# A transformer block's backward pass on one core: sixteen row gathers issued from SyncE's queue, with the order and the homes of buffers searched again

## The chip, the cores and the metric

The kernel runs on one core of a Trainium2 chip. The metric is device time of one execution in microseconds, lower is better. The profile speaks of five engines: PE (TensorE, the matrix multiplier; PEld is its weight load, which overlaps it), DVE (VectorE), ACT (ScalarE), POOL (GpSimd) and SP (SyncE, which computes nothing and only issues transfers). Transfers run on 16 DMA engines that all queues share; "DMA share" is their mean busy time in units of one full set, and can read a little above 1.

## The reference

One block over 2048 rows of 512 numbers in bfloat16, forward and backward: layer norm, attention in which each row looks at 8 rows before it at a distance of 2 (32 heads of 16), a residual, layer norm, a feed-forward net 512 to 1792 to 512 with gelu, a residual. The outputs are the block's result and the gradients of x, wqkv, wo, w1, b1, w2 and b2.

```python
def _A_ref(x, wqkv, wo):
    H = 32; Dh = D // H
    W, dil = 8, 2
    qkv = (x @ wqkv).reshape(B, S, 3, H, Dh).transpose(2, 0, 3, 1, 4)
    q, k, v = qkv[0], qkv[1], qkv[2]
    idx = arange(S)[:, None] - (arange(W) * dil)[None, :]
    mask = idx >= 0
    kg, vg = k[:, :, idx_c], v[:, :, idx_c]
    logits = einsum("bhsd,bhswd->bhsw", q, kg) * Dh ** -0.5
    attn = softmax(where(mask, logits, -1e9))
    o = einsum("bhsw,bhswd->bhsd", attn, vg)
    return o.transpose(0, 2, 1, 3).reshape(B, S, D) @ wo
h = x + _A_ref(layernorm(x), wqkv, wo)
h2 = h + gelu(layernorm(h) @ w1 + b1) @ w2 + b2
# the kernel gives h2 and, for a given grad_out, the gradients of
# x, wqkv, wo, w1, b1, w2, b2
```

## The kernel before

The 2048 rows are cut into four chunks of 512. For each chunk the forward pass makes layer norm, q, k and v, the attention's weights, its output `o`, and the feed-forward net; then come the backward parts of the net, of the attention and of layer norm; products for the weight gradients (`wg_group`) are spread between them and give PE work while others wait.

Nothing in the kernel sets its order by the place in the code. A `Plan` (L62) records 1948 operations, each with an engine, the buffers it reads and writes, and so its predecessors. `emit` (L118) then writes them out in the order of a table, `ORDER`, and lays each buffer at the address that a second table, `HOMES`, gives it. Memory is used many times over: an operation that writes a buffer waits for all that used the same addresses before. Each engine, and SP's and POOL's sequencers among them, runs its own operations strictly in that order. 276 operations are SP's and 33 POOL's.

Attention over 8 rows at distance 2 is done by a *gather* (L456): one transfer that gives each of 128 partitions 18 neighbouring rows of 512 numbers from a tensor in DRAM, 2304 KB in all, as one long piece of 18432 bytes per partition (L460). There are 16: rows of v for the forward output (`Ro`, from `p1_o`, L705, one for each chunk) and, in `p3_bands` (L925), rows of k, go and q for the gradients of q, v and k (`Rq`, `Rv`, `Rk`, one each for each chunk). A gather can leave when its rows stand in DRAM and the memory of its buffer is free. What then uses it is `band` (L501), four times for each gather: DVE multiplies the rows by coefficients (`prbo`, `prbq`, `prbv`, `prbk`, L507), PE sums the products into PSUM (the band sum, L516, eight matmuls with `S4`), ACT writes them out (L521), and `turn` (L525, PE at L532) transposes two of them.

Other names: loads are issued at L282, stores at L287, transposing loads at L291, stores of transposed blocks at L445, all from SP unless they say otherwise. POOL issues, besides the gathers, four stores of `ost` to `o_d` and three stores of `gqs`, `gvs` and `gks` (L287). L297 is ACT's eviction of PSUM. `mmul` is a matmul, as one piece (L270) or as four of 32 columns (L268). `wg_group` (L977) evicts two blocks of a weight gradient into one buffer `wgs` and stores it in 256 KB (`out_dram<-wgs`). `ln1b` (L953) are the rows of layer norm that the last backward part reads, loaded in four pieces per chunk. `ln1T`, `ln2T` and `qt` are transposed rows that feed the matmuls of the first 130 us.

Of the kernel before, what the change touches and what calls it, by code (L numbers as in the profile page):

```python
# [10 lines left out]
P = 128  # L11
# [21 lines left out]
def _ap(apobj, dims, off=0):  # L33
    return bass.AP(tensor=apobj.tensor, offset=apobj.offset + off, ap=[list(d) for d in dims])
# [125 lines left out]
def kernel(  # L160
# [21 lines left out]
    V, A, T, G, SY = nc.vector, nc.scalar, nc.tensor, nc.gpsimd, nc.sync  # L182
# [4 lines left out]
    S, D = xf.shape  # L187
# [11 lines left out]
    RW = 18  # L199
# [44 lines left out]
    sb, ps_, op, fx = pl.sb, pl.ps, pl.op, pl.fixed  # L244
# [211 lines left out]
    def gather(d_b, c, back, tag, soft=()):  # L456
        R = sb("R" + tag, [P, RW, 512])
        r0 = c * CH + (RPAD - 14 if back else 0)
        n = ((c - 1, 1) if c else "b") if back else ((c + 1, 0) if c + 1 < NC else "b")
        op("POOL", 0.58, lambda: G.dma_start(out=R().rearrange("p a d -> p (a d)"), in_=_ap(d_b()[r0:r0 + 1, :], [[4 * D, P], [1, RW * D]])),  # L460
           r=[(d_b, (c, 0)), (d_b, (c, 1)), (d_b, n)] + ([(d_b, (c - 1, 0))] if back and c else []), w=[R], dma=GATHER, tag="gather" + tag, soft=soft, piece=0.8, mode=4)
        return R
# [858 lines left out]
```

## Time and profile before

| | us |
|---|---|
| median of 3 runs | 568.17 (566.8 to 573.35) |
| profiled execution, its own time | 562.53 |
| its span | 560.8 |
| mean granted clock of TensorE | 0.983 |

The profiled execution is one more run; its time is a little below the three others. The span lies 1.7 us inside the time. Of the span, the first 126 us hold the forward pass up to the feed-forward net, then its forward and backward parts follow to about 308 us, then weight gradients of the net with the attention's backward part between them, and from 546 us on the last stores. The transfers by line, with KB and the median from issue to landing:

```profile
Ro<-v_d POOLq DMA_DIRECT2D x4, 2304.0 KB, 11.3
Rq<-k_d POOLq DMA_DIRECT2D x4, 2304.0 KB, 10.9
Rv<-go_d POOLq DMA_DIRECT2D x4, 2304.0 KB, 13.2
```

### The profile page before, as it was taken

To read this page: it belongs to the slowest core of one execution; us is meant where nothing else is said; L and a number is where in the kernel's file an instruction comes from. 1 tells how busy PE (TensorE), PEld (TensorE's weight loads), DVE (VectorE), ACT (ScalarE), POOL (GpSimd) and SP (SyncE) were. 2 spreads that over 40 slices of the span, in tenths; PEclk is the share of its full clock that TensorE was granted. 3 is DMA by queue.
4 is the path that set the end of the run, shared out by engine and by line. 5 is a ranking of instruction groups with operands and counts; after the bars stand their busy time and mean duration, and the time that the engine had idled before them with its cause. 6 is when DMAs were issued, how large, how long until landed. Compare 5 with 4: busy or idle time off the path is not lost. (4 is left out here: it accounts for less than half of the span.)

```text
span 560.8 us, 12918 instructions
## 1 busy us (share of the span) xinstructions
PE 535.7 (96%) x5479; PEld 270.5 (48%) x5512; DVE 494.5 (88%) x649; ACT 306.0 (55%) x480; POOL 24.7 (4%) x38
## 2 busy tenths in 40 slices
PE   8999879999999999999999999999986999999996
PEld 4966434444544444444444444465443554555542
DVE  7999999999999998899895096999984999999984
ACT  3975358988999848892441314213112475554332
POOL 1300100020001000000000000000010001000000
PEclk9999979999999999999999999999997999999999
DMA  8999999998998695669999999999995999659456
GB/s 267 241 318 274 333 280 377 201 285 219 278 221 224 190 238 152 166 150 197 261 187 199 229 202 217 293 200 310 220 399 238 315 315 314 290 197 229 105 145 174
DMA packets 218122, 135.32 MB, mean 241 GB/s; under 512 B 168464, under 2 KB 213712, under 8 KB 216016
## 3 DMA queue, kind: packets, MB, share of 16 engines
q1 hardware_dynamic: 214752, 93.07, 73.0%
q0 software_dynamic: 3312, 41.42, 19.1%
q8 instruction: 43, 0.70, 0.5%
q14 instruction: 15, 0.12, 0.1%
HBM read 55.74 MB, written 39.40 MB: 170 GB/s over the span
## 5 line engine op out<-in xcount | busy, mean ns | idle before, releaser
L270 PE MATMUL ps<-goT,w2T 128*128 128x512 bf16 x220 | 53.5, 379 | 0.5 <-DVE r L699 0.4
L297 ACT CAST wgs<-ps 128x512 bf16<-128x512 f32 (+1 forms) x30 | 16.3, 560 | 66.8 <-PE ps L268 29.0
L270 PE MATMUL ps<-w,gl 128*128 128x512 bf16 x215 | 52.1, 379 | 0.5
L270 PE MATMUL ps<-w1T,xb 128*128 128x512 bf16 x219 | 51.7, 379 | 0.3
L468 DVE TENSOR_TENSOR prb<-got,vw 128x4096 bf16<-128x4096 bf16 x16 | 36.0, 2285 | 16.7 <-ACT got L297 16.4
L270 PE MATMUL ps<-ln2T,w 128*128 128x512 bf16 x192 | 46.8, 390 | 0.3 <-DVE xb L848 0.3
L507 DVE TENSOR_TENSOR prbq<-Rq,cfq 128x4096 bf16<-128x4096 bf16 x16 | 36.1, 2278 | 9.0 <-PE ps L516 7.3
L766 ACT ACTIVATE xb<-ps,b1c 128x512 bf16<-128x512 f32 x56 | 35.4, 693 | 12.5 <-DMA g_d<-gl 9.0
L848 DVE SCALAR_TENSOR_TENSOR xb<-xb,ps 128x512 bf16<-128x512 bf16 x56 | 37.2, 681 | 5.5 <-PE ps L270 4.6
L507 DVE TENSOR_TENSOR prbv<-Rv,cfv 128x4096 bf16<-128x4096 bf16 x16 | 36.0, 2284 | 1.6 <-DMA Rv<-go_d 1.5
L507 DVE TENSOR_TENSOR prbk<-Rk,cfk 128x4096 bf16<-128x4096 bf16 x16 | 35.9, 2286 | 1.5 <-PE ps L516 1.2
L507 DVE TENSOR_TENSOR prbo<-Ro,cfo 128x4096 bf16<-128x4096 bf16 x16 | 36.0, 2285 | 1.2 <-PE ps L476 1.1
L468 DVE TENSOR_TENSOR prf<-qt,kt 128x4096 bf16<-128x4096 bf16 x16 | 35.6, 2282 | 0.0
L270 PEld LDWEIGHTS <-xb 128*128 128x128 bf16 x224 | 21.9, 98 | 26.4
L270 PEld LDWEIGHTS <-gl 128*128 128x128 bf16 x224 | 21.5, 98 | 26.9 <-ACT gl L769 1.0
L270 PEld LDWEIGHTS <-w2T 128*128 128x128 bf16 x220 | 21.4, 98 | 26.8 <-issue 1.5
L616 PE MATMUL ps<-ln1T,wqk 128*32 128x512 bf16 x512 | 31.1, 382 | 1.3 <-DVE ln1T L301 1.0
L270 PE MATMUL ps<-gor,gw2in 128*128 128x512 bf16 x129 | 30.6, 379 | 0.3 <-issue 0.2
L270 PEld LDWEIGHTS <-w 128*128 128x128 bf16 x192 | 19.0, 100 | 24.5 <-issue 3.7
L550 ACT ACTIVATE gyr<-ps,rstd 128x512 bf16<-128x512 f32 x16 | 10.9, 682 | 34.2 <-PE ps L270 34.2
L268 PE MATMUL ps<-gw1in,ln 128*32 128x512 bf16 x464 | 28.8, 396 | 0.0
L788 ACT ACTIVATE xb<-xb 128x2048 bf16<-128x2048 bf16 (+1 forms) x16 | 26.9, 1692 | 2.4 <-DVE xb L787 2.4
(194 smaller groups left out, 1028.4 us busy)
## 6 DMA issues: line engine op xcount, KB each, us to landing
Ro<-v_d POOLq DMA_DIRECT2D x4, 2304.0 KB, 11.3
Rq<-k_d POOLq DMA_DIRECT2D x4, 2304.0 KB, 10.9
Rv<-go_d POOLq DMA_DIRECT2D x4, 2304.0 KB, 13.2
Rk<-q_d POOLq DMA_DIRECT2D x4, 2304.0 KB, 15.0
g_d<-gl SPq DMA_DIRECT2D x9, 512.0 KB, 4.5
gh_d<-xb SPq DMA_DIRECT2D x9, 512.0 KB, 3.8
w<-in_B_w_dram SPq DMA_DIRECT2D x2, 1792.0 KB, 8.9
out_dram<-wgs SPq DMA_DIRECT2D x13, 256.0 KB, 3.3
```

Of the source, the lines that this page charges most:

```text
L268: T.matmul(out[32 * a:32 * a + 32, :], lhsT=l[:, 32 * a:32 * a + 32], rhs=r, start=start, stop=stop, skip_group_check=True)
L270: T.matmul(out, lhsT=l, rhs=r, start=start, stop=stop, skip_group_check=True)
L297: fn = lambda: A.copy(out=ap(), in_=pap())
L468: op("DVE", tt_us(4096), lambda g=g, pr=pr: V.tensor_tensor(out=pr(), in0=ql()[:, g, :].unsqueeze(1).to_broadcast([P, W, 512]), in1=_sub(k ...
L507: V.tensor_tensor(out=pr().rearrange("p a j (d h) -> p a j d h", h=H), in0=_sub(R()[:, o0, 0:1], [[st, 2], [512, 4], [32, DH], [1, H]]), i ...
L550: op("ACT", act_us(D, 1, True), lambda: A.activation(out=gyr()[:, j, :], in_=ps(), func=ACT.Copy, scale=rs[:, t:t + 1], accum_out=sg_[:, i ...
L616: T.matmul(ps()[32 * a:32 * a + 32, gg * 512:(gg + 1) * 512], lhsT=_sub(wq_()[:, dc, 0:1], [[DH, H]], sel * D + 4 * g + a), rhs=rhs, start ...
L766: op("ACT", act_us(512, 1), lambda f=f, ps=ps, xb=xb, f0=f0: A.activation(out=xb()[:, f - f0, :], in_=ps(), func=ACT.Identity, bias=b1c[:, ...
L788: op("ACT", act_us(N), lambda xb=xb: A.activation(out=fl(xb), in_=fl(xb), func=ACT.Tanh, scale=GC), w=[xb], tag="tanh", mode=6)
L848: op("DVE", 0.61, lambda f=f, ps=ps, z=z, f0=f0: V.scalar_tensor_tensor(out=z()[:, f - f0, :], in0=z()[:, f - f0, :], scalar=1.0, in1=ps() ...
```

## The change

The gather's issue moves from POOL to SP. POOL's queue keeps its seven stores.

```diff
-        op("POOL", 0.58, lambda: G.dma_start(out=R().rearrange("p a d -> p (a d)"), in_=_ap(d_b()[r0:r0 + 1, :], [[4 * D, P], [1, RW * D]])),
+        op("SP", 0.58, lambda: SY.dma_start(out=R().rearrange("p a d -> p (a d)"), in_=_ap(d_b()[r0:r0 + 1, :], [[4 * D, P], [1, RW * D]])),
```

Both tables are new as a whole; the 1948 operations, their sizes and what they depend on are the same. Their numbers tell a reader nothing, so one line stands for them:

```diff
 ORDER = (
-    10, 12, 0, 14, 69, 1, 16, 17, 11, 21, 13, 23, 9, 8, 50, 29, 30, 51, 52, 27, 53, 54, 26, 46, 31, 55, 19, 249, 28, 42, 47, 2, 354, 3, 48, 49, 43,
...
```

The places that the prediction speaks of lie in the part with the weight gradients of the feed-forward net. POOL's row before, from the group of three gathers on (rows go by buffer names with numbers that only tell uses apart; `ln_d`, `gq_d`, `k_d` are tensors in DRAM):

```order
L460 DMA Rq_41_4915<-k_d 128x9216
L460 DMA Rk_40_4969<-q_d 128x9216
L287 DMA gq_d<-gqs_38_4500 128x2048
L460 DMA Rv_42_5017<-go_d 128x9216
L287 DMA gv_d<-gvs_43_5088 128x2048
L460 DMA Rq_32_5422<-k_d 128x9216
```

Three gathers stand there with one store between them, and nothing else. SP's row before at the same place, where the fourth line is the store that the prediction takes up:

```order
L282 DMA ro_1439_41_4795<-o_d_69 128x2048
L282 DMA ro_1455_41_4895<-o_d_70 128x2048
L282 DMA ln1b_42_4897<-ln_d_62 32x4x512
L287 DMA out_dram<-wgs_1338_39_4316 128x2x512
L287 DMA out_dram<-wgs_1496_45_5125 128x2x512
```

SP's row now, around the gathers of the same data (`Rq` of chunk 1, `Rk` of chunk 0, `Rv` of chunk 1):

```order
L291 DMA_TRANSPOSE gw1in_36_5103<-gh_d_78 128x4x512
L460 DMA Rq_35_5135<-k_d 128x9216
L460 DMA Rk_35_5138<-q_d 128x9216
L282 DMA ro_1472_36_5150<-o_d_70 128x2048
L287 DMA out_dram<-wgs_1486_40_5191 128x2x512
L282 DMA ro_1508_36_5252<-o_d_71 128x2048
L282 DMA ln1b_37_5254<-ln_d_61 32x4x512 x3
L287 DMA out_dram<-wgs_1471_36_5148 128x2x512
L282 DMA ro_1519_37_5279<-o_d_72 128x2048
L460 DMA Rv_36_5311<-go_d 128x9216
```

`Rq` and `Rk` still leave one behind the other, but `Rv`, before the third of the group, now follows eight instructions later, and the loads and stores of SP stand behind the gathers in the same row.

DVE's products before, which read these gathers:

```order
L507 TENSOR_TENSOR prbq_39_5287<-Rq_41_4915,cfq_41_4982 128x4096
L507 TENSOR_TENSOR prbk_37_5324<-Rk_40_4969,cfk_42_4459 128x4096
L507 TENSOR_TENSOR prbq_32_5366<-Rq_41_4915,cfq_41_4982 128x4096
L507 TENSOR_TENSOR prbk_34_5400<-Rk_40_4969,cfk_42_4459 128x4096
L507 TENSOR_TENSOR prbk_33_5449<-Rk_40_4969,cfk_42_4459 128x4096
L507 TENSOR_TENSOR prbk_33_5498<-Rk_40_4969,cfk_42_4459 128x4096
L507 TENSOR_TENSOR prbv_32_5533<-Rv_42_5017,cfv_37_4373 128x4096
```

and now:

```order
L507 TENSOR_TENSOR prbq_38_5290<-Rq_35_5135,cfq_34_4659 128x4096
L507 TENSOR_TENSOR prbk_35_5309<-Rk_35_5138,cfk_37_5152 128x4096
L507 TENSOR_TENSOR prbk_38_5341<-Rk_35_5138,cfk_37_5152 128x4096
L507 TENSOR_TENSOR prbk_36_5396<-Rk_35_5138,cfk_37_5152 128x4096
L1111 COPY rstdp<-rst 32x16
L507 TENSOR_TENSOR prbk_37_5450<-Rk_35_5138,cfk_37_5152 128x4096
L507 TENSOR_TENSOR prbv_36_5492<-Rv_36_5311,cfv_42_4274 128x4096
```

The products on `Rk` now begin only when all four on `Rq` are through, and those on `Rv` still come last.

201 rows, old and new, of tables (HOMES, ORDER) are left out of this document.

## The prediction

> **What bounds the kernel now.** I read the profile from the whole to the one wait. First the page's engine shares, then the span cut into its stages (each row: the stretch, its length, busy time and count of PE, PEld, DVE, ACT and POOL, the granted clock, the DMA share, GB/s).
>
> ```profile
> span 560.8 us, 12918 instructions
> PE 535.7 (96%) x5479; PEld 270.5 (48%) x5512; DVE 494.5 (88%) x649; ACT 306.0 (55%) x480; POOL 24.7 (4%) x38
> ...
> 0.00:126.00 126.00, 116.35 (x1387) 67.08 (x1392) 119.47 (x154) 85.69 (x110) 14.24 (x21) 0.96 1.05 286
> 126.00:308.00 182.00, 180.45 (x943) 82.44 (x956) 166.51 (x318) 128.45 (x181) 2.47 (x2) 1.00 0.88 206
> 308.00:406.00 98.00, 97.48 (x1129) 49.33 (x1138) 76.49 (x58) 27.07 (x56) 1.66 (x3) 1.00 1.13 238
> 406.00:434.00 28.00, 21.36 (x364) 10.37 (x356) 18.37 (x14) 5.18 (x12) 1.59 (x3) 0.88 0.79 318
> 434.00:546.00 112.00, 110.35 (x1633) 57.10 (x1632) 107.47 (x94) 55.63 (x114) 4.75 (x9) 1.00 0.76 239
> 546.00:560.80 14.80, 9.73 (x45) 4.22 (x44) 6.15 (x14) 3.94 (x12) 0.00 (x0) 0.95 0.66 180
> ```
>
> PE is busy 96% of the span, so an order can win only in the remaining 25.1 us (560.8 - 535.7) and where the clock was low. Three rows hold most of it: the first stretch with 9.65 us (126.00 - 116.35), in which DVE is the fullest engine; the end with 5.07; and 28 us from 406 on, with 6.64 us idle and a clock of 0.88. The third has one cause, and the chain of waits gives it (start, length, what):
>
> ```profile
> 405.50 19.14 DMA out_dram<-wgs
> ...
> 424.75 0.59 ACT wgs L297
> ...
> 425.38 1.05 PE ps L516 x8
> ```
>
> A 256 KB store of weight gradients took 19.14 us to land. ACT could not evict into its buffer (`wgs`), no PSUM came free, and PE's band sum stood. The list of waits (total, times, longest) and the stretch around it show the price:
>
> ```profile
> PE ps L516 <- ACT wgs L297: 6.6, 1, 6.6
> ...
> ACT wgs L297 <- DMA out_dram<-wgs: 11.8, 1, 11.8
> ...
> 422.70:429.53 6.83, 4.15 (x40) 1.79 (x43) 2.29 (x1) 1.57 (x3) 0.00 (x0) 0.50 0.74 315
> ```
>
> The clock was granted at 0.50 for 6.83 us right behind the idle time. Why was the store late? The DMA view of 403 to 425 us (share of 16 engines; KB each; us from issue to landing) and the issues on POOL and SP (start, length, line) answer:
>
> ```profile
> q0 software_dynamic: 500, 6.50, 72.3%
> ...
> Rq<-k_d POOLq DMA_DIRECT2D x1, 2304.0 KB, 12.1
> Rk<-q_d POOLq DMA_DIRECT2D x1, 2304.0 KB, 16.3
> Rv<-go_d POOLq DMA_DIRECT2D x1, 2304.0 KB, 20.8
> ...
> 404.72 0.53 POOL L460 DMA_DIRECT2D Rq<-k_d  x1 [22.56 <-DVE prbv L507]
> 406.54 0.53 POOL L460 DMA_DIRECT2D Rk<-q_d  x1 [1.29 <-PE ps L268]
> ...
> 409.13 0.53 POOL L460 DMA_DIRECT2D Rv<-go_d  x1 [1.53 <-PE ps L516]
> ...
> 405.50 0.60 SPq L287 DMA_DIRECT2D out_dram<-wgs  x1
> ...
> out_dram<-wgs SPq DMA_DIRECT2D x13, 256.0 KB, 3.3
> ```
>
> Three gathers left POOL within 4.4 us of one another, the store left SP between them, and it landed in 19.14 us where the median of 13 such stores is 3.3. POOL's queue held 72.3% of the DMA engines there.
>
> **The change part by part.** The sum is made against the profiled execution, 562.53 us by its own time for a span of 560.8. The median of the runs is 568.17 (566.8 to 573.35), 5.64 above it; I carry the difference over to the median unchanged.
>
> *The stall.* In the new order Rq (chunk 1) and Rk (chunk 0) still leave back to back, but Rv (chunk 1) follows 8 SP instructions later: two `wgs` stores and six loads stand between them and it. The three no longer leave together, and SP issues nothing past an instruction that waits. The price of a gather in the queue: all of POOL's transfers hold 19.1% of 16 engines over 560.8 us, that is 107.1 us, for 41.42 MB, so 2.36 MB (2304 KB) cost 6.1 us.
>
> ```profile
> q1 hardware_dynamic: 214752, 93.07, 73.0%
> q0 software_dynamic: 3312, 41.42, 19.1%
> ```
>
> A `wgs` store right behind two gathers in one queue would land after 2 x 6.1 + 3.3 = 15.5 us at worst. Of the two stores that follow Rq and Rk, the first is ready only after six more groups of four matmuls, a band sum and four turns (7.4 us by the rows below), so it lands within 15.5 - 7.4 = 8.1 us of its issue. The order takes the memory of both again only some 15 us of PE work after their issue; I take both as hidden. Gain: 6.64 us of idle time and the slow clock, half of the 4.15 us that PE was busy at 0.50, 2.07. Together -8.71. (Bounds: 0, if another store or gather is late in its place; -8.71.)
>
> *The load of ln1b.* The list of waits holds one more DMA that PE stood for, in the same part of the program, with this on the chain:
>
> ```profile
> PE ps L270 <- DMA ln1b<-ln_d: 1.1, 1, 1.1
> ...
> 455.62 12.77 DMA ln1b<-ln_d
> ```
>
> The loads of ln1b go on sharing the engines with gathers, now in the same queue. I take 0, bounds -1.1 and, with one 6.1 us gather ahead of it, +6.1.
>
> *The 16 issues.* POOL loses them, SP gains them. Their durations on POOL:
>
> ```profile
> L460 POOL DMA_DIRECT2D Ro<-v_d x4: 533/597/711, 29.1 to 120.5; - x4
> L460 POOL DMA_DIRECT2D Rv<-go_d x4: 527/528/532, 381.6 to 490.3; - x4
> ```
>
> At 0.53 to 0.71 us each that is 8.5 to 11.4 us of SP's sequencer over 560 us. SP computes nothing, so it costs 0 on the path unless what is behind is due at once. POOL does little else (4% busy): 0 there as well.
>
> *The wait that moves to SP.* Here the change does add something. A gather must wait until the memory of its rows is free and the rows stand in DRAM; POOL could stand there for long at no cost:
>
> ```profile
> POOL Rq L460 <- PE ps L268: 167.4, 1, 167.4
> ...
> POOL Ro L460 <- ACT ost L521: 27.0, 1, 27.0
> ```
>
> On SP every load and store behind a waiting gather would stand too. The order answers that by where the gathers stand: Rq and Rk, shown with the change, come right behind a transposed load that waits for PE's work of the same moment, and ahead of loads and stores of which none is due before that. I take 0; the bound above is 6.1 us for each gather that still holds SP up as long as it transfers.
>
> *How late a gather may land.* From the order I counted the PE work between the release of the rows' memory and the first band sum that needs them, and priced it by the chain of waits:
>
> ```profile
> 499.12 2.59 PE ps L268 x48
> 501.71 0.43 PE ps L516 x8
> ...
> 436.81 0.89 PE ps L532 x16
> ```
>
> A group of four matmuls is 0.865 (2.59 / 3), a band sum 0.43, a turn 0.45. The two shortest are Rv of chunk 1, 13 groups and 8 band sums: 14.7 us, less a product (2.28, below) and 0.1 for the hand-over, so it may land after 12.3; and Rk of chunk 1, 14 groups, 4 band sums, 6 turns: 16.5, less one product by which its release is later than PE's place says and the same 2.4: 11.8. All others have 16 us or more. Lone gathers landed in
>
> ```profile
> L507 DVE TENSOR_TENSOR prbk<-Rk,cfk 128x4096 bf16<-128x4096 bf16 x16 | 35.9, 2286 | 1.5 <-PE ps L516 1.2
> ...
> Ro<-v_d POOLq DMA_DIRECT2D x1, 2304.0 KB, 8.3
> Rv<-go_d POOLq DMA_DIRECT2D x1, 2304.0 KB, 9.3
> Rk<-q_d POOLq DMA_DIRECT2D x1, 2304.0 KB, 10.3
> ```
>
> so at 8.3 to 10.3 nothing is lost: 0. No row shows a gather through SP's queue. The slowest median of a kind on the page is
>
> ```profile
> Rk<-q_d POOLq DMA_DIRECT2D x4, 2304.0 KB, 15.0
> ```
>
> and at 15.0 the two would lose 2.7 + 3.2 = 5.9 us. The lone rows are nearest, since no three leave together any more.
>
> Sum: 562.53 - 8.71 = 553.82 for a profiled run, 568.17 - 8.71 = **559.5 us** for the median, 1.5% faster.
>
> **Where a rule speaks against it.** The row is the store's 19.14 us while POOL's queue took 72.3%, and the 3.3 us it usually needs. The Trainium skill, "DMA: Bandwidth & Descriptors", section "Issuing engines are not separate DMA queues", says that transfers started by SyncE or GpSimd run on the same 16 DMA engines and interleave there, so that several issuing engines save only sequencer time. By it, moving the issue moves no byte, the contention stays, and the sum would be 568.2. The trace agrees that both queues share the engines; whether the late store goes by spacing the gathers, no run here shows yet.
>
> **The rivals.** *The gain is given back (within 1%).* The same 41.42 MB go over the same engines in the same time, and the store's wait is followed by another of its kind: either the stall is kept in full, 568.2, or the gathers land at 15.0 and cost 5.9 of the 8.71, 565.4. For it speaks that the stages around are full: the share of DMA is 1.13 from 308 to 406. Against it speaks that the stall hung on three issues within 4.4 us. The first of these two is the outcome that the Trainium skill's rule above would give.
>
> *Slower: head of line on SP's queue in the first stretch.* In the first 126 us four v gathers go out among the loads, stores and transposes which all feed LN, QKV and the weights, and DVE is busy 119.47 of 126, so a late transposed load there can't be made up. Each gather is a block of 6.1 us in the one in-order queue. It decides from 8.71 / 6.1 = 1.4, so two gathers whose block shows make the kernel slower, +3.5 = 571.7; three of the four give +18.3 - 8.7 = +9.6, 577.8. For it: the DMA share in that stretch is 1.05, and the second queue is also full later,
>
> ```profile
> q1 hardware_dynamic: 66996, 19.34, 99.1%
> ```
>
> from 300 to 403 us, without the gathers. Against it: the transfers behind a gather have mostly 8 us and more of PE work before they are used.
>
> **How the numbers follow.** A measurement of this kernel can tell about 1% from no change, so 562.5 and 573.9 are the borders. That the stall goes and nothing takes its place: 0.50, faster. That the gain is given back: 0.28, all of it within 1%, some half of it with the stall kept in full. That SP's queue blocks: 0.22, nearly all beyond +1%, since two blocks give 571.7 and three 577.8. So faster 0.50, same 0.28, slower 0.22. The low end of the range is 551.5: the forecast, less the ln1b wait of 1.1, and less 6.9, which is about half of what else PE stood idle in the first and last stretch (9.65 + 5.07 = 14.72). The high end is 577.8, three blocks. Each end leaves out about 1 in 10. The forecast's own range is 551.5 to 562.5.
>
> **What would show it.** Right: no idle time of PE above 2 us between 400 and 440, no clock of 0.50 there, PE idle for some 16 us in all instead of 25, `wgs` stores landing within 6 us outside the pair Rq, Rk, and lone gathers near 10 us. The head of line would show as SP transposes or loads that land 6 us or more late, with PE or DVE waiting for `ln1T`, `ln2T` or `qt` before 130 us. The given-back gain would show as waits of DVE products for Rv or Rk of chunk 1. Wrong would be the forecast if the gathers landed after more than 12 us when alone, if SP stood behind waiting gathers while loads were due, or if the first stretch grew by more than 6 us.

## The result and the profile after

| | before | changed |
|---|---|---|
| median of 12 runs, us | 567.22 | 565.5 |
| lowest to highest | 559.35 to 593.59 | 563.02 to 568.83 |
| profiled execution: time, span | 562.53, 560.8 | 565.0, 563.2 |
| ratio, with its 95% interval | | 1.0063 (1.0034 to 1.0092) |

The change is a loss of 0.6%, inside the 1% that counts as no change. The median fell by 1.7 us all the same: the ratios here leave out disturbed, longer executions, of which the kernel before has several and the changed one none. The spread fell from 34 us to 6. Before three runs were known, with a median of 568.17; twelve go down to 559.35.

The page of the changed kernel: its shares, its queues, and the gathers at their new issuer (KB each, median us from issue to landing).

```profile
span 563.2 us, 12838 instructions
PE 537.6 (95%) x5482; PEld 265.3 (47%) x5482; DVE 495.8 (88%) x649; ACT 307.4 (55%) x480; POOL 17.7 (3%) x22
...
q1 hardware_dynamic: 217056, 130.82, 89.1%
q0 software_dynamic: 1008, 3.67, 1.7%
...
Ro<-v_d SPq DMA_DIRECT2D x4, 2304.0 KB, 10.2
Rq<-k_d SPq DMA_DIRECT2D x4, 2304.0 KB, 9.2
Rv<-go_d SPq DMA_DIRECT2D x4, 2304.0 KB, 11.1
Rk<-q_d SPq DMA_DIRECT2D x4, 2304.0 KB, 11.3
```

All but POOL's own 3.67 MB are in one queue now, and the gathers land no later than from POOL: the medians were 11.3, 10.9, 13.2 and 15.0. The stages in the columns of the prediction's table:

```profile
0.00:126.00 126.00, 113.92 (x1323) 60.12 (x1324) 116.03 (x148) 85.06 (x105) 13.54 (x17) 0.96 1.00 280
126.00:308.00 182.00, 178.96 (x979) 81.13 (x978) 166.07 (x311) 128.79 (x180) 2.49 (x3) 1.00 0.85 206
308.00:406.00 98.00, 96.49 (x1297) 49.66 (x1299) 75.88 (x63) 27.82 (x59) 0.59 (x1) 1.00 1.08 228
406.00:434.00 28.00, 27.93 (x211) 13.24 (x207) 27.74 (x23) 8.18 (x15) 0.53 (x1) 1.00 1.02 336
434.00:546.00 112.00, 109.01 (x1633) 56.22 (x1626) 104.43 (x94) 54.21 (x115) 0.53 (x1) 1.00 0.77 243
546.00:563.20 17.20, 11.34 (x53) 4.95 (x51) 5.62 (x14) 3.33 (x7) 0.00 (x0) 0.89 0.77 214
```

From 406 to 434 us PE stood 0.07 us in place of 6.64, and the clock was granted in full in place of 0.88. In every other stretch PE stood longer than before: 12.08 against 9.65 in the first, then 3.04 against 1.55, 1.51 against 0.52, 2.99 against 1.65, and 5.86 against 5.07 at the end. Together 25.6 us against 25.1. The stall is gone and the idle time is not. PE's list of waits (total, times, longest) has no late store and no `ln1b` any more, but many small waits:

```profile
PE ps L516 <- DVE prbo L507: 3.6, 3, 1.8
PE ps L270 <- DVE mx L682: 3.1, 3, 2.2
PE ps L270 <- DVE xb L848: 2.2, 2, 1.8
PE ps L270 <- DMA ln2T<-ln: 1.8, 1, 1.8
PE ps L516 <- DVE prbq L507: 1.4, 1, 1.4
```

### The profile page after: what moved, and what is told of

It reads as the page before. It is cut to its first block, busy times and chain, and to the rows that moved or that the text cites. A ratio compares the mean times of both kernels' runs of the same rounds, so it can differ in the third digit from the quotient of the medians.

```text
span 563.2 us, 12838 instructions
## 1 busy us (share of the span) xinstructions
PE 537.6 (95%) x5482; PEld 265.3 (47%) x5482; DVE 495.8 (88%) x649; ACT 307.4 (55%) x480; POOL 17.7 (3%) x22
## 3 DMA queue, kind: packets, MB, share of 16 engines
q0 software_dynamic: 1008, 3.67, 1.7%
## 4 chain that ended last, share of the span: by engine, by line
PE 42%; DVE 13%; DMA 6%; issue 2%; ACT 2%; SPq 1%; DVEq 0%
PE ps L270 31%; PE ps L268 8%; DVE prb L468 4%; DMA out_dram<-wgs 3%; DVE prbq L507 3%; PE ps L516 2%; DMA Rq<-k_d 2%; DMA go_d<-tmgod 1%; DVE prbv L507 1%; SPq L291 1%; ACT woT L1117 1%; DVE xb L795 1%; DVE x L791 1%; DVE cfv L486 1%; PE ps L476 1%
## 5 line engine op out<-in xcount | busy, mean ns | idle before, releaser
L270 PE MATMUL ps<-goT,w2T 128*128 128x512 bf16 x220 | 53.7, 379 | 2.5 <-DVE xb L848 2.2
L270 PE MATMUL ps<-w1T,xb 128*128 128x512 bf16 x224 | 51.8, 379 | 0.0
L270 PE MATMUL ps<-w,gl 128*128 128x512 bf16 x216 | 49.6, 379 | 0.0
L270 PE MATMUL ps<-ln2T,w 128*128 128x512 bf16 x184 | 44.3, 390 | 2.0 <-DMA ln2T<-ln 1.8
L848 DVE SCALAR_TENSOR_TENSOR xb<-xb,ps 128x512 bf16<-128x512 bf16 x56 | 37.1, 680 | 6.1 <-PE ps L270 5.8
L468 DVE TENSOR_TENSOR prb<-got,vw 128x4096 bf16<-128x4096 bf16 x16 | 36.1, 2282 | 1.8 <-PE ps L270 1.0
L468 DVE TENSOR_TENSOR prf<-qt,kt 128x4096 bf16<-128x4096 bf16 x16 | 35.8, 2281 | 1.8 <-PE ps L516 1.8
L270 PEld LDWEIGHTS <-w2T 128*128 128x128 bf16 x220 | 21.4, 98 | 29.2 <-issue 4.3
L270 PEld LDWEIGHTS <-xb 128*128 128x128 bf16 x224 | 21.9, 98 | 26.5 <-issue 0.2
L270 PEld LDWEIGHTS <-gl 128*128 128x128 bf16 x216 | 20.9, 98 | 25.3 <-issue 0.4
L270 PEld LDWEIGHTS <-w 128*128 128x128 bf16 x184 | 18.1, 99 | 25.0 <-issue 5.4
L784 ACT ACTIVATE x<-xb 128x2048 bf16<-128x2048 bf16 (+1 forms) x16 | 26.4, 1691 | 4.5 <-DVE x L792 4.2
L769 ACT ACTIVATE gl<-xb 128x2048 bf16<-128x2048 bf16 (+1 forms) x16 | 27.0, 1693 | 0.1
L616 PEld LDWEIGHTS <-wqk 128*32 128x32 bf16 x512 | 20.6, 140 | 8.4 <-issue 1.7
## 6 DMA issues: line engine op xcount, KB each, us to landing
Ro<-v_d SPq DMA_DIRECT2D x4, 2304.0 KB, 10.2
Rk<-q_d SPq DMA_DIRECT2D x4, 2304.0 KB, 11.3
w<-in_B_w_dram SPq DMA_DIRECT2D x2, 1792.0 KB, 11.8
```

Source lines behind the costliest of these rows:

```text
L270: T.matmul(out, lhsT=l, rhs=r, start=start, stop=stop, skip_group_check=True)
L468: op("DVE", tt_us(4096), lambda g=g, pr=pr: V.tensor_tensor(out=pr(), in0=ql()[:, g, :].unsqueeze(1).to_broadcast([P, W, 512]), in1=_sub(k ...
L616: T.matmul(ps()[32 * a:32 * a + 32, gg * 512:(gg + 1) * 512], lhsT=_sub(wq_()[:, dc, 0:1], [[DH, H]], sel * D + 4 * g + a), rhs=rhs, start ...
L769: op("ACT", act_us(N), lambda xb=xb, gl=gl: A.activation(out=fl(gl), in_=fl(xb), func=ACT.Gelu_apprx_tanh), r=[xb], w=[gl], tag="gelu", mo ...
L784: op("ACT", act_us(N), lambda xb=xb, x2=x2: A.activation(out=fl(x2), in_=fl(xb), func=ACT.Square), r=[xb], w=[x2], tag="x2")
L848: op("DVE", 0.61, lambda f=f, ps=ps, z=z, f0=f0: V.scalar_tensor_tensor(out=z()[:, f - f0, :], in0=z()[:, f - f0, :], scalar=1.0, in1=ps() ...
```

## The experiments

Three theories stood against each other. A: the queue is nearly neutral and the new order's own small waits cost what the stall gave. B: SyncE's in-order queue costs. C: a gather from SyncE's queue is gentler on the other transfers. The order and homes can be taken from either kernel and the issuing engine from the other, since both have the same 1948 operations.

**The old order with the new queue.**

```diff
-        op("POOL", 0.58, lambda: G.dma_start(
+        op("SP", 0.58, lambda: SY.dma_start(
```

in the kernel before, its tables kept.

> The order and homes of before, but all 16 gathers issued by SyncE (one line differs from before). Theory A (the new order's own small waits cost what the stall's end gave; the queue itself is nearly neutral): the time stays within 1% of before, and the wait of PE behind the late weight-gradient store (6.64 us in the profile of before) stays above 3 us, since three gathers still leave together. Theory B (SyncE's in-order queue costs, because transfers stand behind gathers that wait or run): 1 to 4% slower than before, with PE or DVE waiting for transposed loads in the first 126 us. Theory C (a gather issued by SyncE is itself gentler on the stores): 1% faster and more, the store landing within 8 us.

558.77 us, ratio 0.9926 (0.9885 to 0.9967): 0.7% faster than before, short of the 1% that theory C expected, and 6.7 us below the changed kernel (1.4% by the two ratios, 1.0063 / 0.9926). The place of the old stall in its profile, as stage and as a list of issues (start, length) with the landings under it:

```profile
406.00:434.00 28.00, 28.00 (x469) 14.29 (x470) 25.70 (x18) 12.59 (x23) 0.53 (x1) 1.00 0.99 375
...
410.00 0.58 SPq L287 DMA_DIRECT2D out_dram<-wgs  x1
410.68 0.41 SPq L460 DMA_DIRECT2D Rq<-k_d  x1
411.13 0.46 SPq L460 DMA_DIRECT2D Rk<-q_d  x1
411.81 0.32 SPq L460 DMA_DIRECT2D Rv<-go_d  x1
...
Rv<-go_d SPq DMA_DIRECT2D x1, 2304.0 KB, 21.4
out_dram<-wgs SPq DMA_DIRECT2D x1, 256.0 KB, 4.7
```

The three gathers leave within 1.2 us, closer than before, and the third lands after 21.4 us as it did before (20.8). But the store stands ahead of them in the same queue and lands after 4.7 us in place of 19.14. PE doesn't stand at all in that stage. So theory C holds here in its mechanism, and the cure was the store's place in the one queue, not the distance between gathers.

**The new order with the old queue.** The same line the other way, in the changed kernel.

> The order and homes of the changed kernel, but the 16 gathers issued by GpSimd (one line differs from the changed kernel). Theory A (the order makes the difference, the queue is nearly neutral): 563 to 567 us as the changed kernel, no stall at the store. Theory B (SyncE's queue costs): 1% faster than the changed kernel, some 559 us. Theory C (issuing from SyncE is what steadies the transfers): slower than the changed kernel and wider in its runs, over a spread of 15 us between its lowest and highest run, as the kernel before has and the changed one has not.

604.8 us, ratio 1.0508 (1.0422 to 1.0594). Four of the seven executions took 604.8 to 605.39 us and three 590.4 to 592; the ratio goes by the three. Theories A and B fall, since this order is far from indifferent to the queue; C's direction is right, and the spread is the 15 us expected. In the profiled execution, which is one of the longer ones, one place shows how a transfer of the other queue is hurt (issues, landings, then PE's wait):

```profile
76.10 11.40 SPq L291 DMA_TRANSPOSE ln2T<-ln  x1
...
76.33 0.59 POOL L460 DMA_DIRECT2D Ro<-v_d  x1 [4.81 <-PE ps L616]
...
Ro<-v_d POOLq DMA_DIRECT2D x1, 2304.0 KB, 24.9
ln2T<-ln SPq DMA_TRANSPOSE x1, 25.8
...
PE ps L270 <- DMA ln2T<-ln: 22.1, 2, 21.2
```

In the changed kernel the same load stands ahead of the same gather in one queue. There SP issued it in 2.02 us, the gather left behind it, and the load landed after 4.4 us, the gather after 9.9:

```profile
79.27 2.02 SPq L291 DMA_TRANSPOSE ln2T<-ln  x1
81.39 0.84 SPq L460 DMA_DIRECT2D Ro<-v_d  x1
...
Ro<-v_d SPq DMA_DIRECT2D x1, 2304.0 KB, 9.9
ln2T<-ln SPq DMA_TRANSPOSE x1, 4.4
```

**The kernel before once more**, unchanged.

> The kernel before, unchanged, for a second profile and as a null comparison. Ratio 1.00. If the stall of 6.64 us behind the late store belongs to every execution, this profile has it again within 2 us; if it is one case of a collision that comes out otherwise from run to run, the wait differs by over 3 us or stands at another store, and the time follows it (559 us without it, 575 us and above with several).

568.64 us, ratio 1.0048 (0.9995 to 1.0101): half a per cent is what two runs of one kernel can differ by here. The stall changed its victim. The store was late again (25.1 us to landing), but PE stood for two other transfers around 415 us first, and for the eviction 1.6 us only:

```profile
PE ps L268 <- DMA gw1in<-gh_d: 6.6, 1, 6.6
PE ps L268 <- DMA ro<-o_d: 4.5, 1, 4.5
...
PE ps L516 <- ACT wgs L297: 1.6, 1, 1.6
...
406.00:434.00 28.00, 16.95 (x244) 7.17 (x240) 11.83 (x11) 2.53 (x7) 1.58 (x3) 0.76 1.02 342
```

It cost 11.05 us of idle time (28.00 - 16.95) in place of 6.64. In both profiles transfers that left with the three gathers or right behind them were late, and the one that PE waited for differs.

**Which gathers?** Two runs in the old order with a queue chosen by kind:

```diff
+        eng = "POOL" if tag in ("o",) else "SP"
+        op(eng, 0.58, lambda: (G if eng == "POOL" else SY).dma_start(
```

and the same with `("q", "k", "v")`.

> The order and homes of before; the 12 gathers of the attention's backward part (Rq, Rv, Rk) from SyncE, the 4 of v rows from GpSimd. If the gain of SyncE's queue lies at the group of three gathers beside the store: 557 to 560, as with all 16, and no wait for a late store. If it lies in the first stretch: 563 to 568.

557.81 us, ratio 0.9864 (0.9812 to 0.9915): the whole gain, and the lowest median and ratio of this study, though its interval meets that of all 16 gathers from SyncE.

> The order and homes of before; the 4 gathers of v rows from SyncE, the 12 others from GpSimd. The complement of the run above: 562 to 567 and a stall of 5 us or more around 420 us if the gain lies at the group of three; 557 to 560 if it lies in the first stretch.

569.68 us, ratio 1.0102 (1.0054 to 1.0149): worse than the 562 to 567 expected. Its first stretch is as before (PE idle 10.02 us, 126.00 - 115.98); PE stood 4.6 us for the store's eviction beside the group of three, and 10.5 us for the transposing load `gw1in`. That longer wait was over some 16 us before the group left: the load stood beside a lone gather (the chain's piece, then POOL's issues; L461 is L460 of the other kernels).

```profile
385.21 17.12 DMA gw1in<-gh_d
...
385.63 0.53 POOL L461 DMA_DIRECT2D Rv<-go_d  x1 [33.71 <-DVE prbq L508]
417.98 0.53 POOL L461 DMA_DIRECT2D Rq<-k_d  x1 [31.82 <-DVE prbv L508]
```

So the gain lies with the 12 gathers of the backward part, and not at the group of three alone.

**In order within the queue?** The old order with all gathers from SyncE, and one entry of the table moved:

```diff
 ORDER = (
-    ..., 1767, 1731, 1392, 1490, 1267, ...
+    ..., 1767, 1392, 1490, 1267, ..., 1286, ..., 1374, 1731, ...
```

1731 is the store of `wgs`; 1267, 1286 and 1374 are the gathers Rq, Rk and Rv.

> All 16 gathers from SyncE in the order of before, but one instruction is moved: the 256 KB store of weight gradients that stood ahead of the three gathers on SyncE's queue (it landed in 4.74 us there) stands behind the third. If a queue serves its transfers in order, it lands only when the gathers are through, 3 x 5.5 + 3 = 19 us or more after its issue, ACT's eviction into its buffer waits for it, PE stands 6 to 14 us, and the time is 564 to 572 in place of 558.8. If transfers of one queue overtake one another: it lands within 8 us and the time stays at 559.

571.85 us, ratio 1.0124 (1.0082 to 1.0167). As the theory of one queue in order wants it: the store left after the third gather, landed within 1 us behind it (415.30 + 19.4 against 414.93 + 19.0), and PE stood.

```profile
414.93 0.32 SPq L460 DMA_DIRECT2D Rv<-go_d  x1
415.30 0.53 SPq L287 DMA_DIRECT2D out_dram<-wgs  x1
...
Rv<-go_d SPq DMA_DIRECT2D x1, 2304.0 KB, 19.0
out_dram<-wgs SPq DMA_DIRECT2D x1, 256.0 KB, 19.4
...
PE ps L516 <- ACT wgs L297: 10.6, 1, 10.6
```

One row of the table is worth 13 us by the medians (571.85 against 558.77) and 2.0%, some 11 us, by the two ratios (1.0124 / 0.9926). One queue isn't gentler as such. It makes the place in the order decide, and in the old order the places were right. Plain loads gained from being ahead across two queues too: in the profile of before, two loads `ro` that SP issued from 403.89 us on, ahead of POOL's first gather (404.72), landed in 3.6 and 4.7 us, and `ln1b`, behind that gather, in 12.6. Whether the store, put ahead of gathers that stay on POOL, would be in time as well, no run shows.

**Is the new order's spacing worth something without the queue?** The changed kernel with the 12 gathers of the backward part back on POOL, and, apart from it, with the 4 of v rows back on POOL.

> The order and homes of the changed kernel; the 12 gathers Rq, Rv, Rk from GpSimd, the 4 of v rows from SyncE. This tells whether the new order's spacing of the gathers is enough by itself to end the stalls at late stores and loads. If it is, as the prediction assumed: 564 to 567, and PE idle between 350 and 434 us stays below 3 us. If one queue for both is what ends them: 572 to 590 and 8 us or more of idle time there.

587.8 us, ratio 1.0428 (1.0321 to 1.0535). No: PE stood 12.60 us from 308 to 406 (98.00 - 85.40), where the changed kernel has 1.51, and a long wait behind a `wgs` store is there (L477 and L469 are L476 and L468 of the other kernels):

```profile
308.00:406.00 98.00, 85.40 (x1068) 43.59 (x1072) 67.11 (x58) 21.25 (x43) 1.13 (x2) 0.95 0.97 206
...
PE ps L477 <- DVE prb L469: 8.6, 1, 8.6
...
DVE prb L469 <- DMA out_dram<-wgs: 8.8, 1, 8.8
```

The store itself landed in 5.6 us, but it left late: SP took 7.46 us to issue the transposing load ahead of it, beside a lone gather (`Rq`, 357.62 us). Spacing doesn't help against that. In the changed kernel the issue of such a load right behind a gather takes as long (8.19 us, at 367.94 us), where PE doesn't wait for it.

> The order and homes of the changed kernel; only the 4 gathers of v rows from GpSimd, the others from SyncE. With all 16 from GpSimd this order took 605 and PE stood 21.2 us for the transposed load ln2T in the first 126 us, 18 us more in all there than with SyncE. If the order needs the gather behind that load in one queue: some 583 to 588 with that wait again. If the loss was elsewhere: 565 to 570.

571.87 us, ratio 1.0111 (1.0035 to 1.0186), between the two cases expected. Three of its four executions took 569.8 to 572.64; the profiled one, 585.98, has the wait for `ln2T` again, 21.8 us. So that long wait seems to come in some executions only; none of the shorter ones was profiled. Without it the v gathers cost this order some 3 us by the ratios (1.0111 / 1.0063) and 6 by the medians.

**Smaller packets.** The gather from POOL as three transfers of six rows, in both orders:

```diff
+        def go(n=6):
+            for k in range(0, RW, n):
+                G.dma_start(out=R()[:, k:k + n, :].rearrange("p a d -> p (a d)"), in_=_ap(d_b()[r0 + k:r0 + k + 1, :], [[4 * D, P], [1, n * D]]))
+        op("POOL", 0.58, go,
```

> The order and homes of before and GpSimd as the issuer, but each gather goes out as three transfers of six rows (6144 bytes per partition and packet in place of 18432). Theory of turns (the DMA engines take a packet from each queue in turn, so a small packet of SyncE's queue waits for one gather packet each time; 18432 bytes took 0.69 us, so 6144 should take 0.23): the store of weight gradients beside the three gathers has 8 packets of the load ahead of it and 16 of its own on each engine, 24 x (0.23 + 0.05) + 2 = 8.7 us to landing in place of 19.1; its wait goes below 2 us, the time is 1% and more below before, and the runs lie closer together. Theory of bytes (the store is late because so many bytes are in flight): store and stall as before, time within 0.5%.

562.92 us, ratio 1.0014 (0.9969 to 1.0058): no gain, against the theory of turns. The longest landing of a `wgs` store was 15.5 us in the profiled execution, not 8.7; that execution is the longest of its runs (574.76), so it shows a bad case. Its longest wait of PE, 10.2 us, is again for `gw1in` beside a lone gather (`Rv`, 385.37 us), away from the store that the theory spoke of.

> The order and homes of the changed kernel, GpSimd as the issuer, each gather in three transfers of six rows. Theory of turns: PE's wait of 21.2 us for the transposed load ln2T beside the third gather of v rows, which the same order had with whole gathers from GpSimd, falls to 8 us or less, and the time from 605 to 585 or below. Theory of bytes: the wait stays above 15 us and the time above 595.

591.6 us (586.48 to 597.88, four runs). The wait for `ln2T` was 4.5 us at longest, as the theory of turns expected; the time did not reach 585. Since whole gathers seem to have that wait in some executions only, one profile doesn't prove the packets' part in it. Both runs together leave the theory open: smaller packets did not replace the one queue.

**Where does the new order lose?** Two orders were spliced from both tables, all gathers from SyncE. Memory is so full that 375 and 388 of the 855 buffers lie at homes that neither table gives them.

> All gathers from SyncE; the first 550 operations (some 122 us) in the order of before, all others in the order of the changed kernel, homes mended where the two tables meet. The order of before with SyncE's gathers took 558.8, the changed kernel 565.5. If the new order loses its 6.7 us in the first stretch (a head of line on SyncE among loads and transposes): 559 to 561. If it loses them in the later part: 564 to 567. If they are spread: between.

640.6 us, ratio 1.1412 (1.1338 to 1.1486).

> All gathers from SyncE; the first 400 operations (some 88 us) in the order of the changed kernel, all others in the order of before, homes mended where the two tables meet. Loss in the first stretch: 563 to 567. Loss in the later part: 557 to 560. Spread: between.

608.51 us, ratio 1.0852 (1.0788 to 1.0916). Both are far outside all three cases, and both have new waits in most stages, in the first of them with products that wait for a store which still reads their memory (11.0 us for a store of `wgso`, 9.9 for one of `wgs`). They tell nothing of the question, since the order and the mended homes changed together.

Two second profiles, with no change:

> The changed kernel again, for a second profile. Waits that belong to its order come again at the same place within 0.5 us: PE behind the row maximum near 31 us (2.2), behind the transposed load ln2T near 82 us (1.8), behind xb near 280 us (1.8). Waits that are chance differ by more.

564.63 us. The wait behind `xb` near 278 us came again (1.8 us), and those behind the row maximum and `ln2T` changed (1.2 and 1.1 in place of 2.2 and 1.8).

> The order of before with all gathers from SyncE again, for a second profile: its idle time between 126 and 308 us stays below 1 us (0.5 in the first), against 3.0 in the changed kernel, if that part of the loss belongs to the new order; the slow clock in the first 126 us differs from look to look if it is chance.

560.29 us. The stage from 126 to 308 us in the four profiles, the old order first, then the changed kernel:

```profile
126.00:308.00 182.00, 181.48 (x958) 82.62 (x957) 166.97 (x318) 128.96 (x181) 2.53 (x2) 1.00 0.88 207
126.00:308.00 182.00, 180.77 (x945) 82.65 (x957) 168.25 (x321) 130.25 (x181) 2.53 (x2) 1.00 0.88 209
...
126.00:308.00 182.00, 178.39 (x967) 81.15 (x979) 164.51 (x309) 128.52 (x181) 1.98 (x2) 1.00 0.85 203
```

With the changed kernel's first profile (178.96, above): PE idle 0.52 and 1.23 against 3.04 and 3.61 us. The 1.23 misses the expected value below 1. There some 2.4 us belong to the new order, and 2.2 of them are PE's waits for DVE's `xb`, which stand in both lists of the changed kernel with the same numbers (`PE ps L270 <- DVE xb L848: 2.2, 2, 1.8`) and in neither list of the old order with SyncE's queue. At the end of the span it is 0.8 and 1.0 more (5.02 = 9.50 - 4.48 and 5.01 = 12.50 - 7.49 against 5.86 and 6.02 = 16.90 - 10.88). In the first 126 us there is no such difference (12.24 and 13.95 against 12.08 and 13.08).

## Why the prediction was wrong

- **The forecast, 559.5 us and faster:** measured 565.5 and, by the ratio, 0.6% slower. The time lies inside the range (551.5 to 577.8); the direction does not hold. Of the signs named, the clock and the missing stall came; PE's idle time in all did not fall to some 16 us but stayed at 25.6.
- **The stall, -8.71:** right in size at its place (6.64 us to 0.07, the clock from 0.88 to 1.00 in that stage), wrong in its reason. I put it down to the three gathers that "no longer leave together". With the gathers still together the queue alone ended it (4.7 us to landing), and with the spacing alone, on the old queue, PE stood 12.60 us from 308 to 406 us, beside a lone gather.
- **The rest of the order, costed at nothing:** this step failed. The prediction followed the gathers and let all other rows of two wholly new tables count 0. With the same queue, the new order took 565.5 us and the old one 558.77, a loss of 6.7 us or 1.4%, which is more than the queue's gain of 0.7%. In the two pairs of profiles PE stood 3.4 and 3.8 us longer in the new order (25.55 - 22.19 and 29.65 - 25.85). Some 2.4 us of that lie between 126 and 308 us, nearly all in the waits for `xb`, and 0.8 and 1.0 at the end. The rest of the longer span is PE's busy time, 4.3 us in the first pair and 0.6 in the second; no cause for it was shown.
- **From one profile to the median:** the 5.64 us between them were carried over as if they were fixed. They are chance, of the stall at least in part: the runs of before go from 559.35 to 593.59, and two profiles show different victims at the same three gathers. What the change takes away is that spread (34 us, now 6) more than the 8.71 us of one execution.
- **The 16 issues at 0:** right. On SP the four of Rk took 0.32 to 0.54 us each, about the 0.53 of POOL or less, and PE's list of waits names none of them.
- **The wait that moves to SP, and the rival of SP's queue:** no block of 6.1 us showed in the first stretch. PE stood 2.4 us longer there than in the first profile of before, as the old order also does with the same queue (12.24), though not with the four v gathers alone on it (10.02). The rival had the right mechanism at the wrong place: what stands behind gathers in the queue is late by them (19.4 us), but both orders put little there that is due.
- **How late a gather may land:** nearly held. The pair Rq, Rk landed after 9.4 and 15.0 us, the tight Rv and Rk of chunk 1 after 10.3 and 12.4, beside limits of 12.3 and 11.8, so Rk was 0.6 late; DVE stood 2.8, 2.4 and 2.2 us for Rk, Rq and Rv in all, and PE 1.4 at most for a product on one of them.
- **The rule weighed against it:** the Trainium skill, "DMA: Bandwidth & Descriptors", section "Issuing engines are not separate DMA queues", would have the issuer matter for sequencer time alone. Here one line, with the order kept, moved the time by 0.7% in one order and by 4.4% in the other (1.0508 / 1.0063). The measurement decides.
- **The rival "given back within 1%"** is what happened, though through the order's own waits and not through a second late transfer.

The old order with the 12 backward gathers on SyncE, at 557.81 us and a ratio of 0.9864, beats both kernels.

## What to carry to other kernels

Here a large transfer on a queue of its own delayed small transfers that left with it or right behind it, and which one hurt changed from run to run; on the same queue the store was late behind the gathers and in time ahead of them, so put the urgent small ones ahead. When a change brings both a new mechanism and a new schedule, run each with the other's old half before you credit either: here the queue gained 0.7% in the old order and the schedule lost 1.4%. And treat a stall at a contended transfer in one profile as a draw from a spread, not as a constant to subtract.

## What the runs showed of the hardware

While both queues had much to do, their packets shared the DMA engines by number and not by bytes. In the profile of before, from 409 to 424 us, in which the store was on its way all the time (packets, MB, share of 16 engines):

```profile
q0 software_dynamic: 450, 5.59, 92.0%
q1 hardware_dynamic: 413, 0.39, 7.5%
```

450 packets of POOL's queue and 413 of SP's, nearly one for one, while the first moved 14 times the bytes. This fits the Trainium skill, "DMA: Bandwidth & Descriptors", section "Queues, rings and completion order", by which an engine takes the queues in turn, packet by packet. With packets of a third the size a `wgs` store still took 15.5 us in place of 19.1, which speaks against turns as the whole cause. A transposing load beside one gather of the other queue is another case: `ln2T` and `Ro` both took 25 us, and in the run with the v gathers alone on SyncE all queues together moved 60 GB/s from 395 to 400 us, when PE waited for `gw1in`, after 397 from 390 to 395. Why is not known; no run here separates it.
